# Two feed-forward layers behind a retention layer: the place of g's remainder in layer 1, and who copies the finished sums

## The chip, the cores and the metric

The kernel runs on one core of one Trainium2 chip. The metric is the device time of one execution in microseconds (us). Before the change it was 1250.7 us, the median of three runs from 1245.84 to 1251.95. TensorE (PE in the rows; PEld is its loading of weights), VectorE (DVE), ScalarE (ACT) and GpSimd (POOL) work side by side, each through its own list of instructions in order; all transfers of this kernel are issued by SyncE (SP).

## The reference, cut to what matters

```python
def _attn_ref(q, k, v):                      # batch 4, heads 8, seq 768, head_dim 64
    for t in range(S):
        state = gamma * state + einsum('bhd,bhe->bhde', k[:, :, t], v[:, :, t])
        y[:, :, t] = scale * einsum('bhd,bhde->bhe', q[:, :, t], state)

def _moe_ref(x, w_in, w_out, a, b):          # layer 1: 3072 tokens, 512 -> 2048 -> 512
    h = x @ w_in
    P = a[0] + a[1] * h + a[2] * h2 + a[3] * h3
    Q = 1.0 + abs(b[0]) * abs(h) + abs(b[1]) * h2
    g = P / (Q + 1e-06)
    return g @ w_out

def _moe2_ref(x, w_in, w_out):               # layer 2: the same sizes
    h = x @ w_in
    g = h * clip(h + 3.0, 0.0, 6.0) / 6.0
    return g @ w_out

out = _moe2_ref(_moe_ref(attn_out))
```

## The kernel before, in words

The 3072 tokens are cut into six blocks of 512. The retention layer (`att_*`) is computed in chunks of 128 tokens and runs in between layer 1. Each of the two feed-forward layers goes through its hidden units in 16 tiles of 128 (`f`). One **step** is one layer, one block and one tile: `emit_h` makes h, 128 hidden units x 512 tokens, in one PSUM bank; VectorE and ScalarE make g from it; `emit_o` multiplies g with the tile of `w_out` and adds to four PSUM banks, which are the halves of the tiles `accA` and `accB`. Layer 1 is `layer == 0` in the code, layer 2 is `layer == 1`.

All numbers are split into a part that TensorE's fp32r format holds exactly and the rest: x into `xh` and `xl`, weights into `wh` and `wl`, g into `gh` and `gl`. A product is the sum of three: high x high, high x low, low x high. So h takes 12 matmuls of 128x512 (4 slices of the input x 3), and the output takes 12 (4 banks x 3). ScalarE makes `gh` (`s_hi`, L416); VectorE makes `gl` = g - `gh` (`s_lo`, L422).

g of layer 1 takes the following. ScalarE makes three functions of h (`s1_h`, L388 to L390: `p`, `s`, `u`). VectorE makes `p` x h, then `u`, then a last `p` from h (`s1_pq`, L396 to L398). ScalarE takes the logarithm and the exponential of `u` (`s1_r`, L403 and L404). VectorE makes g in three instructions (`s1_g`, L409 to L411). Layer 2 needs one instruction of each engine (L428, L434).

The order of all work is written out by hand in one loop over steps, and each engine keeps it. In turn n of the loop TensorE gets h of step n, then the output matmuls of step n-2; ScalarE and VectorE work on h of step n-1 and finish g of step n-2. Weights come by DMA, and their split is spread over the steps: ScalarE scales (`w_scale`, L110), VectorE takes the bits apart (`w_bits`, L115, L117, L120), ScalarE casts (`w_hi`, L127), VectorE subtracts (`w_lo`, L132). A chunk of retention adds its scores (`sc`, L205) on TensorE in one turn, the mask (`T` or `Tb`, L214) on VectorE and the matmuls `py` (L236 to L262) on TensorE in the next, and ScalarE's copy of `py` (`xh`, L292, or `xf`, L287) in the one behind that.

The steps are ordered in segments: in each layer the first 8 tiles of block 0, then all of block 1, the other 8 tiles of block 0, and blocks 2 to 5. A segment of block 0 leaves its sums in DRAM, and the other adds to them. At the end of a segment `emit_evac` copies the four banks out of PSUM (L365, L369, L371) and sends them to DRAM. Before the change the copies go to ScalarE and VectorE in turn, at the end of the turn of the loop, behind `gl`; and in layer 1 the output matmuls of that turn are held back and issued one turn later, together with the next ones:

```python
        wait = len(late) > 0 and late[0][0] == 0
        for key in late:
            emit_evac(*key)
```

## Time and profile before

| | us |
|---|---|
| median of three runs | 1250.7 |
| the profiled execution | 1249.73 |
| its span, first to last instruction | 1247.9 |
| TensorE busy (matmuls) | 1165.6 (93%) |
| VectorE busy | 837.2 (67%) |
| ScalarE busy | 602.2 (48%) |
| mean share of full TensorE clock | 0.978 |

The share of busy time is a mean over stretches that differ: the first 45 us are mostly transfers and the retention of block 0; up to about 720 us layer 1 runs, with retention beside it up to about 610; then layer 2. Weights are split from 18 to 235 us and from 620 to 830 us. One row of the chain of waits, followed back from the end, has TensorE with 70% of the span and VectorE with 18%. In a row of a timeline the number in brackets is the time in which the engine stood idle before the instruction, and behind the arrow what ended it.

### The profile page before, as it was taken

What the parts mean: (1) busy time and instruction counts of PE and PEld (TensorE: products, weight loads), DVE (VectorE), ACT (ScalarE), POOL (GpSimd) and SP (SyncE); (2) the same over time, 40 slices, a digit from 0 to 9 for tenths busy, and PEclk for the clock granted to TensorE, in tenths of its full rate; (3) what the DMA queues carried; (4) which work ended last, traced back from release to release, by engine and by line L of the source; (5) the groups of instructions that cost most, each with busy time, mean ns of one, the idle gap of its engine ahead of it and who ended that gap; (6) DMA issues with size and microseconds to landing.
All of it is one profiled execution on the core that took longest, in us unless ns stands there. A gap on an engine that the chain in (4) does not pass through costs nothing.

```text
span 1247.9 us, 15484 instructions
## 1 busy us (share of the span) xinstructions
PE 1165.6 (93%) x6022; PEld 940.6 (75%) x6022; DVE 837.2 (67%) x1293; ACT 602.2 (48%) x974; POOL 0.3 (0%) x6
## 2 busy tenths in 40 slices
PE   6677787999999999999989999999999999999998
PEld 4455565788788788778877778888888888888886
DVE  6899889889888888888899988753322223232322
ACT  2465556576566565666677655433222222222222
POOL 0000000000000000000000000000000000000000
PEclk9788899999999999999999999999999999999999
DMA  9633323140221211212122154312100100100000
GB/s 333 210 91 105 119 82 119 51 145 8 82 79 43 77 43 60 83 62 77 34 85 68 51 180 145 98 34 85 41 28 1 59 9 1 60 9 1 34 1 34
DMA packets 54650, 91.27 MB, mean 73 GB/s; under 512 B 4785, under 2 KB 23345, under 8 KB 54577
## 3 DMA queue, kind: packets, MB, share of 16 engines
q1 hardware_dynamic: 54576, 90.29, 22.0%
q8 instruction: 47, 0.77, 0.2%
q14 instruction: 27, 0.21, 0.1%
HBM read 74.54 MB, written 15.73 MB: 72 GB/s over the span
## 4 chain that ended last, share of the span: by engine, by line
PE 70%; DVE 18%; DMA 5%; ACT 4%; issue 2%; SPq 1%; ACTq 0%; DVEq 0%
PE h L317 32%; PE accB L340 17%; PE accA L340 17%; DVE p L396 2%; DVE u L409 2%; DVE p L410 2%; DVE p L411 2%; DVE u L397 2%; PE py L236 1%; DMA rwo<-in_moe_w_out_dram 1%; PE sc L205 1%; DVE rwi L117 1%; DVE gl L422 1%; DMA kv<-in_kv_dram 1%; DVE rwo L117 1%
## 5 line engine op out<-in xcount | busy, mean ns | idle before, releaser
L317 PE MATMUL h<-xh,wi 128*128 128x512 f32 x1536 | 511.6, 395 | 1.7 <-DVE p L398 1.0
L317 PEld LDWEIGHTS h<-xh,wi 128*128 128x128 f32 x1536 | 290.6, 189 | 68.2 <-issue 3.1
L317 PE MATMUL h<-xl,wi 128*128 128x512 f32 x768 | 300.6, 391 | 0.2 <-DVE xl L299 0.2
L434 DVE SCALAR_TENSOR_TENSOR g<-r,h 128x512 f32<-128x512 f32 x96 | 66.1, 689 | 164.5 <-ACT r L428 164.5
L317 PEld LDWEIGHTS h<-xl,wi 128*128 128x128 f32 x768 | 145.4, 189 | 30.0 <-DVE xl L299 0.5
L422 DVE TENSOR_TENSOR gl<-g,gh 128x512 fp32r<-128x512 f32 x96 | 66.4, 692 | 124.8 <-ACT gh L416 124.1
L428 ACT ACTIVATE r<-h,cst 128x512 f32<-128x512 f32 x96 | 66.0, 687 | 168.5 <-PE h L317 168.4
L416 ACT ACTIVATE gh<-g 128x512 fp32r<-128x512 f32 x96 | 60.7, 632 | 174.3 <-PE accB L340 172.2
L340 PE MATMUL accB<-gh,wo 128*128 128x512 f32 x384 | 141.0, 409 | 0.0
L340 PE MATMUL accA<-gh,wo 128*128 128x512 f32 x384 | 137.7, 400 | 1.7 <-ACT gh L416 1.7
L340 PE MATMUL accA<-gl,wo 128*128 128x512 f32 x192 | 80.9, 422 | 49.5 <-DVE gl L422 49.5
L340 PE MATMUL accA<-wo,gh 128*128 128x512 f32 x384 | 118.2, 389 | 0.0
L340 PE MATMUL accB<-wo,gh 128*128 128x512 f32 x384 | 118.2, 389 | 0.0
L403 ACT ACTIVATE r<-u,cst 128x512 f32<-128x512 f32 x96 | 69.3, 722 | 65.4 <-DVE u L397 65.4
L388 ACT ACTIVATE p<-h,ab 128x512 f32<-128x512 f32 x96 | 74.4, 775 | 51.2 <-PE h L317 47.6
L340 PEld LDWEIGHTS accA<-gl,wo 128*128 128x128 f32 x192 | 36.8, 192 | 70.5 <-DVE gl L422 63.8
L340 PEld LDWEIGHTS accB<-gh,wo 128*128 128x128 f32 x384 | 76.6, 200 | 17.1
L340 PEld LDWEIGHTS accA<-gh,wo 128*128 128x128 f32 x384 | 73.7, 192 | 17.1 <-ACT gh L416 2.8
L340 PEld LDWEIGHTS accB<-wo,gh 128*128 128x128 f32 x384 | 72.1, 188 | 15.1
L340 PEld LDWEIGHTS accA<-wo,gh 128*128 128x128 f32 x384 | 72.1, 188 | 14.9
L422 DVE TENSOR_TENSOR gl<-p,gh 128x512 fp32r<-128x512 f32 x96 | 65.9, 686 | 24.7 <-ACT gh L416 24.6
L340 PE MATMUL accB<-gl,wo 128*128 128x512 f32 x192 | 78.8, 410 | 0.0
(73 smaller groups left out, 1498.2 us busy)
## 6 DMA issues: line engine op xcount, KB each, us to landing
rwi<-in_moe_w_in_dram SPq DMA_DIRECT2D x32, 512.0 KB, 3.7
rwo<-in_moe_w_out_dram SPq DMA_DIRECT2D x32, 512.0 KB, 3.6
T<-in_qk_t_dram SPq DMA_DIRECT2D x32, 256.0 KB, 3.6
kv<-in_kv_dram SPq DMA_DIRECT2D x32, 256.0 KB, 4.6
x<-o SPq DMA_DIRECT2D x24, 256.0 KB, 2.3
xr<-x SPq DMA_DIRECT2D x24, 256.0 KB, 3.9
out_dram<-o SPq DMA_DIRECT2D x20, 256.0 KB, 2.2
Tr<-in_kv_dram SPq DMA_DIRECT2D x16, 256.0 KB, 6.1
```

The source lines that it names most:

```text
L117: nc.vector.tensor_scalar(out=halves[:, :, 1], in0=halves[:, :, 3], scalar1=-(2**15), scalar2=None, op0=ALU.bitwise_and)
L317: nc.tensor.matmul(ps, lhsT=w[:, cs], rhs=x[:, c, :], start=n == 0, stop=n == 3 * KD - 1)
L340: nc.tensor.matmul(ps, lhsT=l, rhs=r, start=f == f0 and i == 0, stop=f == f1 and i == 2)
L388: nc.scalar.activation(p, h, AF.Identity, scale=ab[:, 3:4], bias=ab[:, 2:3])
L396: nc.vector.tensor_tensor(out=p, in0=p, in1=h, op=ALU.mult)
L397: nc.vector.scalar_tensor_tensor(out=u, in0=s, scalar=babs[:, 1:2], in1=u, op0=ALU.mult, op1=ALU.add)
L403: nc.scalar.activation(r, u, AF.Ln, scale=1.0 / LN_SCALE, bias=ln_bias)
L409: nc.vector.scalar_tensor_tensor(out=u, in0=u, scalar=Q_CONST, in1=r, op0=ALU.add, op1=ALU.mult)
L416: nc.scalar.activation(gh, tm[key], AF.Copy)
L422: nc.vector.tensor_tensor(out=gl, in0=tm.pop(key), in1=gh.bitcast(F32), op=ALU.subtract)
L428: nc.scalar.activation(r, hps[key], AF.Relu, bias=three)
L434: nc.vector.scalar_tensor_tensor(out=g, in0=r, scalar=6.0, in1=h, op0=ALU.min, op1=ALU.mult)
```

## The change

Four things are altered.

- `emit_h`: the 12 matmuls run through the four slices of high x high first, then high weight x low x, then low weight x high x. Before, each slice had its three products together.
- `emit_o`: in layer 1 the matmuls run over all four banks with one product after the other, and those with `gl` come last. In the last step of a segment, and in layer 2, each bank still gets its three products together, but with `gl` as the third.
- `s1_pq` takes a function that it calls between `u` and the last `p`; in layer 1 this is `s_lo` of the step before, which used to come behind `s1_r`.
- In layer 1 all four copies are on ScalarE, emitted right behind `s1_h` (for a segment that adds to sums from DRAM they stay on VectorE, and are emitted behind `gh`). The holding back of output matmuls is gone.

TensorE's order at the turn in which step 4 of block 1 gets its output matmuls: `h_1_6` is h of step 6 in block 1, `accA` and `accB` are the four banks, `py_1` the retention matmuls of chunk 1. Before:

```order
L317 MATMUL h_1_6_1369<-xh_455,wi_6_685 128x512
L340 MATMUL accA_1_0_1226<-gh_1_4_1391,wo_4_629 128x512 [waits Activation_49]
L340 MATMUL accA_1_0_1226<-gl_1_4_1406,wo_4_629 128x512 [waits DVE_49]
L340 MATMUL accA_1_0_1226<-gh_1_4_1391,wo_4_629 128x512 x2
L340 MATMUL accA_1_0_1226<-gl_1_4_1406,wo_4_629 128x512
L340 MATMUL accA_1_0_1226<-gh_1_4_1391,wo_4_629 128x512
L340 MATMUL accB_1_0_1227<-gh_1_4_1391,wo_4_629 128x512
L340 MATMUL accB_1_0_1227<-gl_1_4_1406,wo_4_629 128x512
L340 MATMUL accB_1_0_1227<-gh_1_4_1391,wo_4_629 128x512 x2
L340 MATMUL accB_1_0_1227<-gl_1_4_1406,wo_4_629 128x512
L340 MATMUL accB_1_0_1227<-gh_1_4_1391,wo_4_629 128x512
L236 MATMUL py_1_1423<-T_1_1216,kv_1_1217 64x128 [waits DMAHW0_49,DVE_49]
```

The same turn after the change:

```order
L317 MATMUL h_1_6_1369<-xh_455,wi_6_685 128x512 x4
L341 MATMUL accA_1_0_1148<-gh_1_4_1391,wo_4_629 128x512 [waits Activation_49]
L341 MATMUL accA_1_0_1148<-gh_1_4_1391,wo_4_629 128x512
L341 MATMUL accB_1_0_1149<-gh_1_4_1391,wo_4_629 128x512 x2
L341 MATMUL accA_1_0_1148<-gh_1_4_1391,wo_4_629 128x512 x2
L341 MATMUL accB_1_0_1149<-gh_1_4_1391,wo_4_629 128x512 x2
L341 MATMUL accA_1_0_1148<-gl_1_4_1402,wo_4_629 128x512 [waits DVE_49]
L341 MATMUL accA_1_0_1148<-gl_1_4_1402,wo_4_629 128x512
L341 MATMUL accB_1_0_1149<-gl_1_4_1402,wo_4_629 128x512 x2
L236 MATMUL py_1_1423<-T_1_1230,kv_1_1231 64x128 [waits DMAHW0_49,DVE_49]
```

The first matmul that waits for `gl` (DVE) was the second of twelve, and is the ninth.

VectorE's order in the same turn, from the first instruction on h of step 5 to the mask. Before:

```order
L396 TENSOR_TENSOR p_5_1384<-p_5_1384,h_1_5_1307 128x512
L397 SCALAR_TENSOR_TENSOR u_5_1383<-s_5_1382,babs,u_5_1383 128x512
L398 SCALAR_TENSOR_TENSOR p_5_1384<-p_5_1384,ab,h_1_5_1307 128x512 [waits DVE_49]
L422 TENSOR_TENSOR gl_1_4_1406<-p_4_1322,gh_1_4_1391 128x512 [waits PE_49]
L214 TENSOR_TENSOR T_1_1216<-sc_1_1360,tab 128x1024 [waits DMAHW7_49,PE_49]
```

After the change:

```order
L397 TENSOR_TENSOR p_5_1384<-p_5_1384,h_1_5_1307 128x512
L398 SCALAR_TENSOR_TENSOR u_5_1383<-s_5_1382,babs,u_5_1383 128x512
L425 TENSOR_TENSOR gl_1_4_1402<-p_4_1322,gh_1_4_1391 128x512 [waits PE_49]
L401 SCALAR_TENSOR_TENSOR p_5_1384<-p_5_1384,ab,h_1_5_1307 128x512 [waits DVE_49]
L214 TENSOR_TENSOR T_1_1230<-sc_1_1360,tab 128x1024 [waits DMAHW7_49,PE_49]
```

`gl` has changed places with the last `p`; the mask `T_1` stands where it stood.

ScalarE's order around the end of the first segment, where `o_0_7_0` to `o_0_7_3` are the copies of the four banks, `p_1`, `s_1`, `u_1` the functions of h of step 1 in block 1, and `gh_1_0` the cast of g of step 0. Before:

```order
L388 ACTIVATE p_1_1109<-h_1_1_1032,ab 128x512 [waits DVE_49,PE_49]
L389 ACTIVATE s_1_1107<-h_1_1_1032 128x512
L390 ACTIVATE u_1_1108<-h_1_1_1032,ab 128x512
L416 ACTIVATE gh_1_0_1116<-p_0_1047 128x512 [waits DVE_49]
L110 ACTIVATE rwo_10_1071<-rwo_10_1071 128x512 [waits DMAHW6_49]
L127 ACTIVATE wo_10_1123<-rwo_10_1071 128x512 [waits DVE_49]
L403 ACTIVATE r_1_1128<-u_1_1108,cst 128x512 [waits DVE_49,Activation_49]
L404 ACTIVATE r_1_1128<-r_1_1128 128x512 [waits Activation_49]
L369 ACTIVATE o_0_7_0_1133<-accA_0_0_552 128x512 [waits PE_49]
L369 ACTIVATE o_0_7_2_1139<-accB_0_0_553 128x512 [waits PE_49]
L388 ACTIVATE p_2_1188<-h_1_2_1094,ab 128x512 [waits DVE_49,PE_49]
```

After the change:

```order
L389 ACTIVATE p_1_1109<-h_1_1_1032,ab 128x512 [waits DVE_49,PE_49]
L390 ACTIVATE s_1_1107<-h_1_1_1032 128x512
L391 ACTIVATE u_1_1108<-h_1_1_1032,ab 128x512
L370 ACTIVATE o_0_7_0_1113<-accA_0_0_552 128x512 [waits PE_49]
L370 ACTIVATE o_0_7_1_1116<-accA_0_0_552 128x512
L370 ACTIVATE o_0_7_2_1119<-accB_0_0_553 128x512 [waits PE_49]
L370 ACTIVATE o_0_7_3_1122<-accB_0_0_553 128x512 [waits DMAHW7_49,Activation_49]
L419 ACTIVATE gh_1_0_1128<-p_0_1047 128x512 [waits DVE_49]
L110 ACTIVATE rwo_10_1071<-rwo_10_1071 128x512 [waits DMAHW6_49]
L127 ACTIVATE wo_10_1135<-rwo_10_1071 128x512 [waits DVE_49]
L406 ACTIVATE r_1_1142<-u_1_1108,cst 128x512 [waits DVE_49]
L407 ACTIVATE r_1_1142<-r_1_1142 128x512 [waits Activation_49]
```

Two copies behind the exponential have become four behind the functions of h, in front of the cast `gh_1_0` and of the scaling of the next weight.

```diff
--- before.py
+++ after.py
@@ -310,12 +310,11 @@
         ps = ps_h.tile([128, 512], F32, tag="h", name=f"h{layer}_{blk}_{f}")
         wh, wl = weights["wi", layer, f]
         xh, xl = xin[blk + layer * NBLK]
-        n = 0
-        for c in range(KD):
+        pairs = ((wh, xh), (wh, xl), (wl, xh))
+        for n, (i, c) in enumerate((i, c) for i in range(3) for c in range(KD)):
+            w, x = pairs[i]
             cs = slice(c * 128, (c + 1) * 128)
-            for w, x in ((wl, xh), (wh, xl), (wh, xh)):
-                nc.tensor.matmul(ps, lhsT=w[:, cs], rhs=x[:, c, :], start=n == 0, stop=n == 3 * KD - 1)
-                n += 1
+            nc.tensor.matmul(ps, lhsT=w[:, cs], rhs=x[:, c, :], start=n == 0, stop=n == 3 * KD - 1)
         hps[key] = ps
 
     def emit_o(key):
@@ -329,15 +328,17 @@
                 for t in (ps_acc.tile([128, 1024], F32, tag=f"acc{s}", name=f"acc{s}{layer}_{blk}_{f}") for s in "AB")
                 for i in range(2)
             ]
-        for j in range(KD):
+
+        parts = [(i, j) for i in range(3) for j in range(KD)]
+        if layer == 1 or f == f1:
+            parts.sort(key=lambda t: t[1])
+        for i, j in parts:
             js = slice(j * 128, (j + 1) * 128)
-            ps = acc[layer, blk][j]
             if layer == 0:
-                terms = ((wl[:, js], gh), (wh[:, js], gl), (wh[:, js], gh))
+                l, r = ((wh[:, js], gh), (wl[:, js], gh), (wh[:, js], gl))[i]
             else:
-                terms = ((gl[:, js], wh), (gh[:, js], wl), (gh[:, js], wh))
-            for i, (l, r) in enumerate(terms):
-                nc.tensor.matmul(ps, lhsT=l, rhs=r, start=f == f0 and i == 0, stop=f == f1 and i == 2)
+                l, r = ((gh[:, js], wh), (gh[:, js], wl), (gl[:, js], wh))[i]
+            nc.tensor.matmul(acc[layer, blk][j], lhsT=l, rhs=r, start=f == f0 and i == 0, stop=f == f1 and i == 2)
 
     partial = {}
 
@@ -365,7 +366,7 @@
                 nc.vector.scalar_tensor_tensor(out=o, in0=ps, scalar=scale, in1=o, op0=ALU.mult, op1=ALU.add)
             else:
                 o = out_tile(layer, blk, j, f"o{layer}_{blk}_{f}_{j}")
-                if j % 2 == 0:
+                if layer == 0 or j % 2 == 0:
                     nc.scalar.activation(o, ps, AF.Copy, scale=scale)
                 else:
                     nc.vector.tensor_scalar(out=o, in0=ps, scalar1=scale, scalar2=None, op0=ALU.mult)
@@ -390,11 +391,13 @@
         nc.scalar.activation(u, h, AF.Abs, scale=ab[:, 4:5])
         tm[key] = [s, u, p]
 
-    def s1_pq(key):
+    def s1_pq(key, between=None):
         s, u, p = tm[key]
         h = hps.pop(key)
         nc.vector.tensor_tensor(out=p, in0=p, in1=h, op=ALU.mult)
         nc.vector.scalar_tensor_tensor(out=u, in0=s, scalar=babs[:, 1:2], in1=u, op0=ALU.mult, op1=ALU.add)
+        if between:
+            between()
         nc.vector.scalar_tensor_tensor(out=p, in0=p, scalar=ab[:, 1:2], in1=h, op0=ALU.add, op1=ALU.mult)
 
     def s1_r(key):
@@ -630,7 +633,7 @@
                 if fn is not att_load:
                     begun.append((fn, *args))
 
-    late, held_back = [], []
+    late = []
     for n in range(len(steps) + LAG):
         cur, k1, k2 = (at_step(n - i) for i in range(3))
         todo = w_until(n) - made["bits"]
@@ -641,6 +644,9 @@
         begun.clear()
         if k1:
             (s1_h, s2_h)[k1[0]](k1)
+        for key in late:
+            if key[:2] not in partial and key[0] == 0:
+                emit_evac(*key)
         for fn, *args in begin.get(n, ()):
             fn(*args)
         if k2 and k2[0] == 0:
@@ -648,23 +654,23 @@
             s_hi(k2)
         elif k2:
             s_lo(k2)
+        for key in late:
+            if key[:2] in acc:
+                emit_evac(*key)
+        late.clear()
         while made["lo"] < made["bits"]:
             w_second()
+        rest = (lambda: s_lo(k2)) if k2 and k2[0] == 0 else None
         if k1 and k1[0] == 1:
+            if rest:
+                rest()
             s2_g(k1)
             s_hi(k1)
         if todo > 0:
             w_first()
         if k1 and k1[0] == 0:
-            s1_pq(k1)
+            s1_pq(k1, rest)
             s1_r(k1)
-        if k2 and k2[0] == 0:
-            s_lo(k2)
-
-        wait = len(late) > 0 and late[0][0] == 0
-        for key in late:
-            emit_evac(*key)
-        late.clear()
         if todo > 1:
             w_second()
         for fn, *args in before.get(n, ()):
@@ -680,13 +686,9 @@
         w_ahead(NW if n < N1 - FT else 2 * NW)
         o = at_step(n - LAG)
         if o:
-            held_back.append(o)
-        if not wait:
-            for o in held_back:
-                emit_o(o)
-                if o[2] == ends[o][1]:
-                    late.append(o)
-            held_back.clear()
+            emit_o(o)
+            if o[2] == ends[o][1]:
+                late.append(o)
         for fn, *args in after.get(n, ()):
             fn(*args)
         if cur and cur[1:] == (0, FT - 1):
```

## Rows read from the trace of the kernel before

**Rows 1.** Busy time in six stretches: length, PE, PEld, DVE, ACT, POOL, clock, DMA

```profile
40.00:127.00 87.00, 63.68 (x355) 47.63 (x348) 82.50 (x134) 50.55 (x84) 0.00 (x0) 0.85 0.37 116
127.00:227.00 100.00, 77.36 (x450) 59.47 (x449) 83.95 (x134) 57.71 (x95) 0.00 (x0) 0.94 0.35 109
227.00:613.00 386.00, 379.88 (x2216) 307.03 (x2215) 330.74 (x504) 239.92 (x389) 0.00 (x0) 1.00 0.20 65
613.00:721.00 108.00, 97.95 (x410) 76.63 (x408) 101.79 (x162) 76.55 (x126) 0.00 (x0) 0.98 0.20 62
721.00:767.00 46.00, 45.40 (x193) 37.40 (x194) 39.69 (x65) 25.78 (x44) 0.00 (x0) 0.96 0.48 164
767.00:1248.00 481.00, 476.15 (x2100) 393.62 (x2098) 169.16 (x254) 142.25 (x225) 0.00 (x0) 1.00 0.11 37
```

**Rows 2.** Waits over the whole span: us in total, times, longest us

```profile
PE accA L340 <- DVE gl L422: 49.5, 29, 3.6
```

**Rows 3.** TensorE's waits from 300 to 600 us

```profile
PE accA L340 <- DVE gl L422: 6.1, 6, 1.3
```

**Rows 4.** VectorE's waits from 127 to 227 us

```profile
DVE rwi L117 <- ACT rwi L110: 6.5, 5, 3.4
```

**Rows 5.** Timeline, 178 to 188 us: start, length, engine, line, what, [idle before]

```profile
178.84 0.74 DVE L398 SCALAR_TENSOR_TENSOR p<-p,ab,h 128x512 f32<-128x512 f32 x1
...
179.50 0.68 DVE L422 TENSOR_TENSOR gl<-p,gh 128x512 fp32r<-128x512 f32 x1
...
180.10 1.22 DVE L214 TENSOR_TENSOR T<-sc,tab 128x1024 f32<-128x1024 f32 x1
...
183.71 1.09 PE L236 MATMUL py<-T,kv 128*64 128x128 f32 x16
...
185.93 0.60 ACT L287 ACTIVATE xf<-py 128x512 f32<-128x512 f32 x1 [2.99 <-PE py L262]
...
187.64 0.76 DVE L117 TENSOR_SCALAR rwi<-rwi 128x512 int16<-128x512 int16 x1 [3.40 <-ACT rwi L110]
```

**Rows 6.** Timeline, 215 to 223 us

```profile
215.70 1.22 DVE L214 TENSOR_TENSOR T<-sc,tab 128x1024 f32<-128x1024 f32 x1
...
220.78 0.60 ACT L287 ACTIVATE xf<-py 128x512 f32<-128x512 f32 x1 [3.05 <-PE py L262]
...
222.50 0.75 DVE L117 TENSOR_SCALAR rwo<-rwo 128x512 int16<-128x512 int16 x1 [2.65 <-ACT rwo L110]
```

**Rows 7.** Timeline, 134 to 146 us, the first end of a segment

```profile
134.23 0.76 ACT L388 ACTIVATE p<-h,ab 128x512 f32<-128x512 f32 x1
...
137.72 0.74 DVE L117 TENSOR_SCALAR rwo<-rwo 128x512 int16<-128x512 int16 x1 [0.34 <-ACT rwo L110]
...
141.84 0.58 ACT L369 ACTIVATE o<-accA 128x512 f32<-128x512 f32 x1
...
142.31 0.59 ACT L369 ACTIVATE o<-accB 128x512 f32<-128x512 f32 x1
...
142.45 0.69 DVE L371 TENSOR_SCALAR o<-accA 128x512 f32<-128x512 f32 x1 [0.74 <-ACT o L369]
...
144.56 0.69 DVE L371 TENSOR_SCALAR o<-accB 128x512 f32<-128x512 f32 x1 [1.42 <-DMA x<-o]
...
145.17 1.21 DVE L214 TENSOR_TENSOR T<-sc,tab 128x1024 f32<-128x1024 f32 x1
```

**Rows 8.** DMA issues: what, count, KB each, median us to landing

```profile
x<-o SPq DMA_DIRECT2D x24, 256.0 KB, 2.3
```

**Rows 9.** Timeline at 226.55 us

```profile
226.55 0.50 PE L340 MATMUL accA<-gl,wo 128*128 128x512 f32 x1 [2.65 <-DVE gl L422]
```

**Rows 10.** The stretch right behind it, columns as in rows 1

```profile
228.00:231.40 3.40, 3.40 (x9) 2.63 (x9) 3.37 (x7) 1.69 (x3) 0.00 (x0) 0.50 0.00 0
```

**Rows 11.** Timeline at the change of layers, 720 to 722 us

```profile
720.87 0.68 DVE L422 TENSOR_TENSOR gl<-p,gh 128x512 fp32r<-128x512 f32 x1
...
721.61 0.50 PE L340 MATMUL accA<-gl,wo 128*128 128x512 f32 x1 [2.36 <-DVE gl L422]
```

## Prediction

> **What bounds the kernel now.** I read the stretches first [rows 1]. Five of them count here. From 40 to 227 us VectorE sets the pace: it is busy 82.5 of 87 us and then 84.0 of 100 us, while TensorE is busy only 63.7 and 77.4. (Neighbouring VectorE instructions overlap by some 0.08 us, so these sums are a little high: 179.50 + 0.68 against a next start of 180.10 [rows 5].) From 227 to 613 TensorE is busy 379.9 of 386 us and sets the pace. From 613 to 721 VectorE does so again, with 101.8 of 108 us. From 721 on TensorE is close to full, and after 767 it is full: 2100 matmuls in 481 us, which is 0.229 us for one. In that last stretch nothing can be gained except by doing fewer matmuls, and the change keeps their number.
>
> Then the waits: TensorE waits 49.5 us in 29 places for `gl`, the rest of g [rows 2], but only 6.1 us of that lies in 300 to 600 [rows 3]. This is the main reading. Where VectorE has no idle time, TensorE's wait is only the other side of VectorE's work, and letting TensorE run past it shortens nothing until VectorE waits in turn for something that TensorE hands over. So I do not count the 49.5 us; I look for places where VectorE itself stands still, and for the places where the pace goes from VectorE to TensorE.
>
> **The change part by part.** Three edits act together in layer 1. (a) In every step but the last of a segment, the output matmuls take `gl` as the last 4 of 12 and no longer as the second. (b) `gl` is made one VectorE instruction earlier, ahead of the third function of h. (c) The finished sums are copied by ScalarE alone, right behind the functions of h, and the next output matmuls are no longer held back by a step. The number of matmuls, and of VectorE instructions in a step without an end, stays. The new order inside h costs nothing that I can see: TensorE never waits there for a weight's low half. At each of the six whole ends of layer 1 two copies leave VectorE, and two are added on ScalarE.
>
> *40 to 127 us.* VectorE is full and nothing is taken from it. Gain 0.
>
> *127 to 227 us.* Here VectorE does wait, mainly for ScalarE's scaling of the next weight; the costliest group of its waits there is 6.5 us in 5 [rows 4]. The long ones come from one chain: `gl`, the output matmuls, the retention matmuls `py` behind them, ScalarE's copy `xf` of `py`, then ScalarE's cast of g and the scaling. At 187.64 VectorE stands 3.40 us for it [rows 5]. By (b) `gl` starts 0.66 us earlier (178.84 to 179.50), and by (a) 4 instead of 11 matmuls are left behind it, which is 7 x 0.229 = 1.60 us. Together 2.26 us, if nothing else holds `py`. The mask `T` is the other input: it starts at 180.10, is 1.22 us long and so ends at 181.32, and `py` starts at 183.71, so there are 2.39 us of room and all 2.26 count. At the second such place [rows 6] the mask ends at 215.70 + 1.22 = 216.92, and `py`, which takes as long as before (183.71 to 185.93, 2.22 us), started at 220.78 - 2.22 = 218.56. There only 1.6 us can be had; I take 1.35 of them for the start of a matmul behind a wait. Sum 3.6.
>
> The first end lies here too [rows 7]. Today VectorE stands behind the copies, 1.42 us of it for a transfer to leave an output buffer, and the mask starts only at 145.17. After the change the four copies stand on ScalarE between the functions of h (from 134.23, about 2 us long) and the cast of g. Two copies start 0.47 us apart, so four take 1.9 us, and the fourth must wait until the first one's transfer has landed, 2.3 us behind its issue [rows 8], about 1.7 us more than its turn. The scaling behind them, and with it VectorE's 137.72, come some 2.7 us later than now. In exchange VectorE is rid of the 1.42 us, of 0.74 us in front of its first copy and of two copies that hold it for 0.6 us each: 3.4 us. Net 0.7 us, and `py` no longer runs in front of a held-back output step. I take 1.2, between 0 and 3.
>
> *227 us, where the pace goes over to TensorE.* From 226.55 on TensorE runs without a wait; it starts there behind 2.65 us of waiting [rows 9]. With 8 of the 12 matmuls done before `gl` it has a lead of 2.26 us over today. VectorE must follow through the next steps; it has idle time there, but not at once. I take 1.9. Right behind it TensorE has its clock at half (0.50, the level of 1.2 GHz) for 3.4 us [rows 10], which costs 1.7 us; in front of the fall it had waited 2.65 us. A shorter wait may spare the fall.
>
> *227 to 613 us.* Only the waits count: 6.1 us in 6 places [rows 3], two at the beginning of each block of tokens, all of them from copies on VectorE and the step held back. With the copies on ScalarE, finished 1.9 us behind the functions of h, and 1.6 us of new room for `gl`, I take all of them away, and the slow start behind each (about 0.1 us): 6.5. The cover for the copies is `py`, for which ScalarE waits at these three ends anyway. Without that cover, 3 x 1.9 = 5.7 us of them return.
>
> *613 to 721 us.* VectorE paces. At the end in this stretch two copies leave it, but the four on ScalarE hold up the scaling for which it waits. I take 0, between -1 and 2.
>
> *721 us, the change of layers.* `gl` of the last step now stands behind a weight's conversion and starts at 720.87; TensorE waits 2.36 us for it and goes on at 721.61 [rows 11]. After the change `gl` of this step comes before that conversion (three instructions) and the next layer's g. Four VectorE instructions of about 0.6 us make 2.4 us, of which I take 2.2 because the cast of g has to be ready, and one more matmul is done before `gl`. From there TensorE has hardly a wait, so 2.5 us are kept. A mean clock of 0.96 in the next 46 us [rows 1] is another 1.8 us that may be spared.
>
> For the two falls of the clock together (1.7 + 1.8) I count a quarter, 0.9. Sum: 3.6 + 1.2 + 1.9 + 6.5 + 0 + 2.5 + 0.9 = 16.6. The profiled execution took 1249.7 us (span 1247.9 and 1.8 around it), 1.0 below the median of the runs. 1249.7 - 16.6 = 1233.1, forecast **1233**.
>
> **Rivals.** *The gain stays in the TensorE-paced part.* VectorE eats what the chains give back, because each stretch it paces ends when its own work ends. Then only 6.5 stay: 1249.7 - 6.5 = 1243. For it speaks that VectorE is busy 84 to 95% in these stretches; against it the 3.40 us idle, which can't be VectorE's work.
>
> *All waits for `gl` go.* 1249.7 - 49.5 = 1200. Against it stands that VectorE has only 4.5 us free of 87 between 40 and 127, and 6.2 of 108 between 613 and 721, so the TensorE waits there have nowhere to go.
>
> *The copies hold up ScalarE (slower).* Place: the six ends. Price: 1.9 us each in front of the cast of g, and 1.7 once for the landing, 13.1 us. It decides if the copies end later than TensorE reaches the next output matmuls, two groups of 12 (5.5 us) behind the end of h. Then the terms 1.2, 6.5 and 2.5 are lost as well and only 3.6 and 1.9 stay: 1249.7 - 5.5 + 13.1 = 1257. Against it: the functions of h and four copies are together about 4 us, below the 5.5.
>
> *The rotation over four banks lowers the clock (slower).* Today six matmuls in a row go to accA, six to accB, and TensorE's clock is 1.00 over 227 to 613 [rows 1]; afterwards each matmul of an output step in layer 1 goes to another bank than the one before. If that left gaps and took the clock to the 0.94 of 127 to 227, some 6% of 386 us would be lost: 1249.7 - 10.1 + 23 = 1263. No row shows a gap where accB follows accA. The Trainium skill (TensorE: Matmul & The Clock Gate, section on a second HAM failure mode) reports a kernel that cycles through PSUM banks each iteration and whose clock went back and forth because of small idle times between groups. By that rule this rival would be the likely one; the trace of before, which already uses four banks in each step at a clock of 1.00, doesn't bear it out.
>
> *The change doesn't do what it says:* if `gl` were late by more than the 1.6 us everywhere, the result would lie within 1249 to 1251.
>
> **How the numbers follow.** Forecast 0.68, gain only in the TensorE-paced part 0.16, all waits 0.03, copies hold up ScalarE 0.07, banks and clock 0.03, no effect 0.03. The forecast's own terms run from 12 (first end 0, handover 1, no clock, a second chain at 1) to 24 us (both falls spared, first end 3, 613 to 721 at 2), that is 1226 to 1238. Taking in the first rival the range is 1224 to 1244. About 0.5% (6 us) is what a measurement can tell from no change. Faster by more: nearly all of the forecast, two thirds of the first rival and all of the second, 0.81. Within 0.5%: 0.11. Slower: 0.08.
>
> **What would show it.** In the profile after, the six `gl` waits of TensorE between 300 and 600 us should be nearly gone, and VectorE's wait at about 187 should be near 1.1 us. The stretch from 40 to 127 should be as long as now. TensorE should go on at the change of layers some 16 us earlier. No ScalarE copy should be the last thing that VectorE or TensorE waits for, except once at the first end. It is wrong if ScalarE's cast of g shows up as what TensorE waits for, if the clock falls inside 227 to 613, or if VectorE's idle time between 127 and 227 stays at its sum.

## The result, and the profile after

The changed kernel takes 1231.07 us (median of four runs, 1229.19 to 1232.37), the kernel before 1249.84 in the same runs. The ratio is 0.9849 (95% interval 0.9828 to 0.987): 18.8 us less. The profiled execution took 1232.37 us, with a span of 1230.6.

Where the time went is read best from the turns of the loop. A turn is taken to begin where ScalarE starts its first function of h (`p`, or `r` in layer 2); the table subtracts these starts. For the changed kernel there are two profiles, the second of them from the experiments. A segment's end, where sums are copied, is called an end; a `py` chain is the way from `gl` over the output matmuls and `py` to the scaling of the next weight; the handover is the place near 227 us where the pace goes from VectorE to TensorE.

| turns | in before, us | length before | after | after, second profile | gain | predicted |
|---|---|---|---|---|---|---|
| up to turn 0 | 0 to 41 | 40.74 | 43.43 | 40.55 | -2.69 (+0.19) | - |
| 0 to 8 | 41 to 127 | 86.40 | 86.32 | 86.38 | 0.08 | 0 |
| 8 to 11, the first end | 127 to 156 | 28.75 | 26.40 | 26.40 | 2.35 | 1.2 |
| 11 to 19, two `py` chains | 156 to 227 | 70.73 | 67.32 | 66.83 | 3.41 | 3.6 |
| 19 to 24, the handover | 227 to 259 | 32.00 | 29.06 | 29.08 | 2.94 | 1.9 and clock |
| 24 to 80 | 259 to 613 | 354.49 | 346.21 | 346.21 | 8.28 | 6.5 |
| 80 to 96 | 613 to 717 | 103.41 | 103.66 | 103.74 | -0.25 | 0 |
| 96 to 108, the change of layers | 717 to 784 | 67.36 | 64.16 | 64.18 | 3.20 | 2.5 |

From turn 108 on both have 451.52 us to their last step. The gains sum to 20.0; less the 2.69 us by which the first profile reached turn 0 later, that is 17.3, the difference of the spans.

TensorE's waits over the whole span, the lines that answer to [rows 2] (us in total, times, longest):

```profile
PE accA L341 <- DVE gl L425: 25.6, 22, 2.8
PE py L236 <- DVE Tb L214: 15.3, 8, 4.4
PE accA L341 <- ACT gh L419: 13.8, 11, 3.4
```

`gl` fell from 49.5 to 25.6 us. From 300 to 600 us, where [rows 3] has 6.1 us, no wait of TensorE is listed any more. What is left lies where VectorE paces, and there part of it only changed its name: TensorE now stands at `gh`, the cast, 13.8 us (1.7 before).

The stretches, with the columns of [rows 1]:

```profile
40.00:127.00 87.00, 64.56 (x393) 47.93 (x392) 82.51 (x134) 50.11 (x83) 0.00 (x0) 0.90 0.36 115
227.00:613.00 386.00, 384.36 (x2249) 312.72 (x2248) 331.69 (x509) 253.05 (x410) 0.00 (x0) 1.00 0.20 67
613.00:721.00 108.00, 99.83 (x416) 77.43 (x416) 102.60 (x164) 76.01 (x126) 0.00 (x0) 0.98 0.26 83
```

VectorE is as busy in the first and third as before (82.5 and 101.8). In the second TensorE has gone from 379.9 to 384.4 of 386 us, with a clock of 1.00.

The first `py` chain, to set beside [rows 5]:

```profile
179.25 0.68 DVE L425 TENSOR_TENSOR gl<-p,gh 128x512 fp32r<-128x512 f32 x1
179.85 0.74 DVE L401 SCALAR_TENSOR_TENSOR p<-p,ab,h 128x512 f32<-128x512 f32 x1
180.51 1.21 DVE L214 TENSOR_TENSOR T<-sc,tab 128x1024 f32<-128x1024 f32 x1
...
181.81 1.09 PE L236 MATMUL py<-T,kv 128*64 128x128 f32 x16
...
184.03 0.60 ACT L287 ACTIVATE xf<-py 128x512 f32<-128x512 f32 x1 [1.49 <-PE py L262]
...
185.73 0.75 DVE L117 TENSOR_SCALAR rwi<-rwi 128x512 int16<-128x512 int16 x1 [1.07 <-ACT rwi L110]
```

VectorE's wait is 1.07 in place of 3.40 us. The mask `T` ends at 180.51 + 1.21 = 181.72 and `py` starts at 181.81: the mask is now what `py` waits for, as the row of its weight load says:

```profile
181.81 0.85 PEld L236 LDWEIGHTS py<-T,kv 128*64 128x64 f32 x16 [0.35 <-DVE T L214]
```

The first end, to set beside [rows 7]:

```profile
138.51 1.09 ACT L370 ACTIVATE o<-accA 128x512 f32<-128x512 f32 x2
140.74 1.09 ACT L370 ACTIVATE o<-accB 128x512 f32<-128x512 f32 x2 [1.14 <-PE accB L341]
141.73 0.62 ACT L419 ACTIVATE gh<-p 128x512 fp32r<-128x512 f32 x1
142.25 0.65 ACT L110 ACTIVATE rwo<-rwo 128x512 f32<-128x512 f32 x1
...
142.93 0.75 DVE L117 TENSOR_SCALAR rwo<-rwo 128x512 int16<-128x512 int16 x1 [2.99 <-ACT rwo L110]
```

VectorE stands 2.99 us for the scaling behind the four copies; ScalarE stands 1.14 us between the second and the third because `accB` was not done. The transfer that held up an output buffer before [rows 7] no longer shows. `accB` was late because TensorE stood for `gl` in the output step of this end and then ran at half its clock. The kernel before waits as long there, and its clock stays full. Before, then after, each with the stretch around it (columns of [rows 1]):

```profile
134.16 0.50 PE L340 MATMUL accA<-gl,wo 128*128 128x512 f32 x1 [2.69 <-DVE gl L422]
134.00:138.50 4.50, 4.34 (x29) 3.40 (x30) 3.84 (x8) 3.27 (x6) 0.00 (x0) 1.00 0.00 0
```

```profile
136.07 0.79 PE L341 MATMUL accA<-gl,wo 128*128 128x512 f32 x1 [2.69 <-DVE gl L425]
136.00:140.50 4.50, 4.43 (x10) 3.14 (x10) 3.66 (x7) 3.57 (x7) 0.00 (x0) 0.50 0.12 45
```

VectorE stands as long at the end near 605 us, where a weight is split in the same turn (1.21 us before, at 621.49):

```profile
609.08 0.76 DVE L117 TENSOR_SCALAR rwi<-rwi 128x512 int16<-128x512 int16 x1 [3.17 <-ACT rwi L110]
```

The change of layers [rows 11], and the clock there:

```profile
704.49 0.69 DVE L425 TENSOR_TENSOR gl<-p,gh 128x512 fp32r<-128x512 f32 x1
704.51 0.73 PE L341 MATMUL accA<-gh,wo 128*128 128x512 f32 x2 [1.84 <-ACT gh L419]
```

```profile
705.00:709.00 4.00, 4.00 (x12) 3.01 (x11) 3.78 (x7) 2.54 (x5) 0.00 (x0) 0.57 0.38 131
```

TensorE resumes 17.1 us earlier than in [rows 11], and waits for the cast, no longer for `gl`. The clock still falls to half there. The fall behind the handover [rows 10] is gone; the one at the first end is new.

### The profile page after: what moved, and what is told of

It is laid out like the page before. It is cut to its first block, busy times and chain, and to the rows that moved or that the text cites. A ratio compares the mean times of both kernels' runs of the same rounds, so it can differ in the third digit from the quotient of the medians.

```text
span 1230.6 us, 15579 instructions
## 1 busy us (share of the span) xinstructions
PE 1161.1 (94%) x6022; PEld 937.6 (76%) x6022; DVE 826.4 (67%) x1281; ACT 609.8 (50%) x986; POOL 0.3 (0%) x6
## 4 chain that ended last, share of the span: by engine, by line
PE 76%; DVE 16%; ACT 4%; issue 2%; DMA 2%; SPq 0%; ACTq 0%; DVEq 0%
PE h L317 35%; PE accA L341 18%; PE accB L341 18%; PE py L236 2%; PE sc L205 2%; DVE p L397 2%; DVE u L398 2%; DVE u L412 1%; DVE p L413 1%; DMA rwo<-in_moe_w_out_dram 1%; DVE rwi L117 1%; DVE p L414 1%; DVE rwo L117 1%; PE py L262 1%; DVE p L401 1%
## 5 line engine op out<-in xcount | busy, mean ns | idle before, releaser
L317 PE MATMUL h<-xh,wi 128*128 128x512 f32 x1536 | 417.8, 394 | 0.7 <-ACT xh L292 0.7
L317 PEld LDWEIGHTS h<-xh,wi 128*128 128x128 f32 x1536 | 286.6, 189 | 65.0 <-issue 3.4
L317 PE MATMUL h<-xl,wi 128*128 128x512 f32 x768 | 206.4, 391 | 0.0
L341 PE MATMUL accA<-gh,wo 128*128 128x512 f32 x384 | 122.0, 399 | 13.8 <-ACT gh L419 13.8
L341 PE MATMUL accB<-gh,wo 128*128 128x512 f32 x384 | 121.0, 397 | 0.0
L341 PE MATMUL accA<-gl,wo 128*128 128x512 f32 x192 | 64.4, 411 | 25.6 <-DVE gl L425 25.6
L341 PEld LDWEIGHTS accB<-gh,wo 128*128 128x128 f32 x384 | 73.6, 192 | 15.9
L419 ACT ACTIVATE gh<-p 128x512 fp32r<-128x512 f32 x96 | 60.7, 632 | 34.5 <-DVE p L414 34.4
L341 PE MATMUL accA<-wo,gl 128*128 128x512 f32 x192 | 74.8, 390 | 0.0
```

Source lines behind the costliest of these rows:

```text
L317: nc.tensor.matmul(ps, lhsT=w[:, cs], rhs=x[:, c, :], start=n == 0, stop=n == 3 * KD - 1)
L341: nc.tensor.matmul(acc[layer, blk][j], lhsT=l, rhs=r, start=f == f0 and i == 0, stop=f == f1 and i == 2)
L419: nc.scalar.activation(gh, tm[key], AF.Copy)
```

## The experiments

Four kernels undo one part of the change each, three make one part alone, one repeats the changed kernel, three go further, and one leaves work out.

**gl second of twelve again** (layer 1):

```diff
-        if layer == 1 or f == f1:
-            parts.sort(key=lambda t: t[1])
+        parts.sort(key=lambda t: t[1])
...
-                l, r = ((wh[:, js], gh), (wl[:, js], gh), (wh[:, js], gl))[i]
+                l, r = ((wl[:, js], gh), (wh[:, js], gl), (wh[:, js], gh))[i]
```

> The changed kernel, but in layer 1 the output matmuls again take the three products of a bank together, with gl second of twelve; the earlier gl and the copies on ScalarE stay. Theory (gl's place among the matmuls counts where a chain runs through them, not between 227 and 613 us): in the trace after, gl is ready 2.4 to 4.3 us before TensorE needs it between 264 and 600 us, and 7 x 0.229 = 1.60 us of that go, so no wait returns there. Back come 1.6 us at each of the two py chains before 227 us (3.2), 1.9 at the handover and perhaps the half-speed clock behind it (up to 1.7), 0.2 at the layer change: 5 to 7 us slower than the changed kernel's 1231, so 1236 to 1238. Rival 1 (the place does the work between 227 and 613 as well): the 6.5 us return too, 1243 to 1245. Rival 2 (the earlier gl and the copies do it all): 1231.

1234.11 us, ratio to the kernel before 0.9873 (0.9851 to 0.9896). Turns 24 to 80 stay at 346.21, so rival 1 falls. The handover costs 2.31 us, and the wait and the half clock are back:

```profile
225.36 0.50 PE L340 MATMUL accA<-gl,wo 128*128 128x512 f32 x1 [1.98 <-DVE gl L424]
```

```profile
227.00:230.40 3.40, 3.40 (x10) 2.64 (x9) 3.37 (x6) 1.69 (x4) 0.00 (x0) 0.52 0.17 66
```

The two chains cost 0.93 and 0.92 us by their turns (13 and 14, 17 and 18), not 3.2 together: the earlier `gl` and the copies cover the rest. The first end costs 1.37 us (turns 8 to 11). The change of layers is 1.34 us shorter than in the changed kernel: the clock does not fall there (1.00 from 705 to 709 us). So the median is 3.0 us above the changed kernel's, less than I expected.

**gl made late again:**

```diff
-            s1_pq(k1, rest)
+            s1_pq(k1)
             s1_r(k1)
+        if k2 and k2[0] == 0:
+            s_lo(k2)
```

(and the call of `rest()` at the change of layers goes.)

> The changed kernel, but gl is made where it was: behind the last p and, at the change of layers, behind the weight's conversion. Theory: 0.66 us return at the first py chain, at most 0.6 at the second, 0.7 at the handover, and 2.2 at the change of layers: 3.5 to 4.5 us slower than the changed kernel, about 1235. No wait of TensorE for gl between 300 and 600. Rival (the order of the matmuls alone does it, and gl's place on VectorE counts for nothing): 1231 to 1232.

1234.3 us, 0.9883 (0.9859 to 0.9907). 2.28 us return at the change of layers and 0.68 at the first end, nothing at the handover. At the first chain `py` starts 1.06 us into its turn instead of 1.09: no loss. At the second it starts 1.77 in instead of 1.08: 0.69, as the 0.66 of `gl`'s place.

**Copies and held-back step as before:** the old `emit_evac`, its old place and `held_back` are put back in.

> The changed kernel, but the finished sums are again copied by ScalarE and VectorE in turn at the end of the turn, and the output matmuls behind an end are held back by a turn. The prediction's step (the copies on VectorE and the held-back step make the waits between 300 and 600; without them they go): 4 to 6.5 us return there and about 2 at the first end, 1237 to 1240. Rival (the 2.26 us of room that gl has won cover these waits of 0.75 to 1.29 us by themselves, so copies and order each do the same work twice over): between 227 and 613 nothing returns, only the first end's 0 to 2.5 us, so 1231 to 1234.

1236.51 us, 0.9898 (0.9877 to 0.9919). 2.18 us return at the first end, 3.03 between turns 24 and 80. That is neither expectation. No wait for `gl` returned between 296 and 613 us; another did:

```profile
PE accA L341 <- ACT gh L419: 1.7, 4, 0.9
```

With `gl` out of the way the cast is late next. Two of the four waits (0.19 and 0.27 us, at 317 and 323) come behind VectorE's copies, from which it works without a pause to g. In front of the other two (0.92 at 426 and 0.37 at 527) VectorE last stood for transfers of the retention's inputs, 0.24 and 0.67 us the one time, 0.47 the other; the changed kernel shows no such wait between 296 and 600 us.

**The old order inside h:** only the loop in `emit_h` is put back.

> The changed kernel, but the 12 matmuls of h are in their old order (the three products of a slice together). Theory: nothing depends on it, 1231. Rival (the new order of h costs the 2.7 us by which the changed kernel's profile reaches its first step later, 43.43 against 40.74 us): 1228 to 1229, and the first step starts near 40.7 us again.

1230.26 us, 0.9848 (0.9823 to 0.9873), the same as the changed kernel within the noise. Its first turn starts at 43.61, so the rival falls.

**The changed kernel again.**

> The changed kernel once more, on the same chip as the three below. Its median should lie within 1229 to 1233. Question beside it: is the later first step (43.43 us instead of 40.74) part of the change or variation? Theory (variation: the code up to there is the same but for the order of h): the first step starts anywhere between 40.5 and 44 us. Rival (part of the change): 43 to 44 us again.

1231.54 us (1229.21 to 1232.88), 0.9847 (0.9828 to 0.9865). Turn 0 starts at 40.55: the start is variation.

**One part alone, added to the kernel before:** the order of the output matmuls, the copies, or `gl`'s place.

> The kernel before with one part of the change: in layer 1 the output matmuls run over the four banks and gl comes last (and gl third in each bank elsewhere). gl's place on VectorE, the copies and the held-back step are as before. Theory (each part covers what another would cover too): between 227 and 613 us 4 to 5 us go, because 1.6 us of room are more than each of the waits of 0.75 to 1.29; 2.5 to 3.5 us at the chains in 127 to 227, 2.3 at the handover, nothing at the first end, 0 to 0.4 at the change of layers: 9 to 11 us in all, so about 1240. Rival (the parts add up: what the order gives alone is what its absence cost, 3.0 us): about 1247.

> The kernel before with the other part: copies by ScalarE alone right behind the functions of h, no held-back step; gl second of twelve and made late, the matmuls in their old order. Theory (each part covers what another would cover too): the whole 8 us between 227 and 613 go, because without the copies VectorE never falls behind; 1.5 to 2.5 at the first end; 0 to 1.5 at the chains; nothing at the handover; -1 to 1 at the change of layers: 9 to 12 us in all, about 1239. Rival (the parts add up: what its absence cost, 5.4 us): about 1244. Rival 2 (the copies on ScalarE hold up the cast of g when gl has no room): slower than 1247.

> The kernel before with gl's new place on VectorE alone (between u and the last p, and ahead of the weight's conversion at the change of layers); matmuls and copies as before. Undone in the changed kernel it cost 3.2 us, 2.3 of them at the change of layers. Theory (0.66 us earlier counts wherever nothing else covers it): six waits of TensorE between 300 and 600 us shrink by 0.66 us each, 4.0; 0.66 at each of the two py chains; 0.7 at the handover; 2.3 at the change of layers: 7 to 9 us, 1241 to 1243. Rival (the place counts at the change of layers alone): 2 to 3 us, about 1247.

| us gained against before, by profile | all | order alone | place alone | copies alone | all but order | all but place | all but copies |
|---|---|---|---|---|---|---|---|
| turns 8 to 11 | 2.35 | -0.26 | -0.31 | 0.19 | 0.98 | 1.67 | 0.17 |
| 11 to 19 | 3.41 | 3.45 | 2.06 | 0.76 | 2.08 | 3.81 | 3.65 |
| 19 to 24 | 2.94 | 2.90 | 1.89 | 0.00 | 0.63 | 2.91 | 2.93 |
| 24 to 80 | 8.28 | 4.68 | 2.14 | 8.28 | 8.28 | 8.27 | 5.25 |
| 96 to 108 | 3.20 | 0.51 | 2.59 | 2.27 | 4.54 | 0.92 | 3.22 |
| median, us | 1231.07 | 1240.01 | 1243.95 | 1242.24 | 1234.11 | 1234.3 | 1236.51 |

Their ratios are 0.9915 (0.9899 to 0.9931), 0.9952 (0.9934 to 0.997) and 0.993 (0.9915 to 0.9945). The three medians alone are 10.4, 6.3 and 8.1 us below the kernel before in their own runs, 24.8 together against 18.8 for the whole; undone one at a time they cost 3.0, 3.2 and 5.4, or 11.7. The parts cover for one another: 10.4 us for the order is the theory's figure, not the 3.0 of simple adding up; the copies (8.1) lie between the 9 to 12 of the theory and the 5.4 of adding up, the place just short of its 7 to 9. (One execution can differ from the median of its kernel by 2 to 3 us, so the stage sums don't give the medians.) In turns 24 to 80, where the clock is 1.00 throughout, the covering is plain: the copies alone take everything. With the place alone the waits between 296 and 613 us only shrink, and a new name appears:

```profile
PE accA L341 <- DVE gl L425: 3.2, 6, 0.7
PE accA L341 <- ACT gh L419: 0.4, 1, 0.4
```

At the first end no part alone does anything. The copies count there together with another part, 1.67 us with the order and 0.98 with the place, and all three give 2.35.

Two rows of the table hold the clock too. At the change of layers it falls in the kernel before, in the changed one, in order alone and in all but place; in the other four it doesn't. The copies alone gain 2.27 us there with TensorE's wait as it was and the fall missing:

```profile
713.53 0.50 PE L341 MATMUL accA<-gl,wo 128*128 128x512 f32 x1 [2.33 <-DVE gl L425]
714.00:718.00 4.00, 4.00 (x20) 3.28 (x19) 3.07 (x6) 2.89 (x7) 0.00 (x0) 1.00 0.40 146
```

The kernel before, behind its 2.36 us [rows 11]:

```profile
722.00:726.00 4.00, 4.00 (x13) 3.16 (x12) 3.13 (x6) 0.58 (x2) 0.00 (x0) 0.61 0.00 0
```

At the handover the clock falls in the kernel before, in copies alone and in all but order. With the place alone it doesn't, behind the same wait as in all but order (1.98):

```profile
227.03 0.50 PE L341 MATMUL accA<-gl,wo 128*128 128x512 f32 x1 [1.96 <-DVE gl L425]
228.40:231.80 3.40, 3.40 (x17) 2.81 (x16) 3.37 (x7) 1.82 (x4) 0.00 (x0) 1.00 0.20 75
```

These two kernels differ in turns 19 to 24 by 1.89 - 0.63 = 1.26 us. They have different copies, which alone give 0.00 there, and a different order inside h, which changes nothing there (29.06 and 29.11 us). So, as an estimate, some 1.3 us of the gain at the handover are the fall that is spared. Whether a kernel shows a fall in every execution was not measured; the changed kernel's two profiles agree.

(In turns 11 to 19 some 0.5 us differ between executions of one kernel, by when a weight's transfer lands: VectorE's wait for it in turn 11 is 0.85 in one profile of the changed kernel and 0.38 in the other.)

**Copies behind the scaling** where a weight is split in the same turn:

```diff
+                if todo > 0:
+                    emit_evac(*key, range(2 if key[1] == 0 else 0))
+                    copies = lambda key=key: emit_evac(*key, range(2 if key[1] == 0 else 0, KD))
...
         w_scale_next(i + 2)
+        if copies:
+            copies()
         w_hi(*jobs[i])
```

> The changed kernel, but at the two ends where a weight is split in the same turn (the first end, and the one at 605 us) copies are moved behind gh and the scaling of that weight: the last two of four at the first end, all four at the other. In the trace after, VectorE waits 2.99 us and 3.17 us there for the scaling, in stretches that VectorE paces. Theory (VectorE's standstill behind the copies is lost time): VectorE's waits fall to about 1.9 and 1.2, and the time falls by 2 to 4 us, to 1227 to 1229. Rival (TensorE is behind at these places anyway, so the waits only move): same time as the changed kernel on this chip.

1229.37 us, 0.9833 (0.9816 to 0.9849); the medians differ by 2.2 us, but the intervals overlap. By profile 1.8 us go at the end near 605 (3.17 becomes 1.21). At the first end the wait moved a turn on, and turns 8 to 11 stay at 26.28 us:

```profile
142.79 0.75 DVE L117 TENSOR_SCALAR rwo<-rwo 128x512 int16<-128x512 int16 x1 [0.75 <-ACT rwo L110]
...
154.00 0.75 DVE L117 TENSOR_SCALAR rwi<-rwi 128x512 int16<-128x512 int16 x1 [3.15 <-ACT rwi L110]
```

**gl last at the ends too**, on top of that: `if layer == 1 or f == f1:` becomes `if layer == 1:`.

> The kernel with the copies behind the scaling (the run before), and gl last over all four banks in the last step of a segment of layer 1 too. In the trace of the run before, VectorE's standstill at the first end went from 2.99 to 0.75 us, but 3.15 us came in the next turn, for a scaling that waits for the retention matmuls py; TensorE had stood 2.69 us at the ending step's gl with 8 matmuls ready that need no gl, and then ran 12 matmuls, scores, h and an output step without a pause up to py. Theory (TensorE's lateness at the first end is that order): 2 to 2.8 us go in the turns 8 to 11, nothing between 227 and 613, 0 to 1 at the change of layers; 1226 to 1228 where the changed kernel has 1231.5. Rival (the copies, which can begin only when all banks are done, hold up gh and the scaling by what is won): 1229 to 1230.

1227.66 us (1225.41 to 1228.08), 0.982 (0.9803 to 0.9837), the fastest kernel here. Turns 8 to 11 are 24.16 us, 2.24 below the changed kernel, and both waits are short:

```profile
140.72 0.75 DVE L117 TENSOR_SCALAR rwo<-rwo 128x512 int16<-128x512 int16 x1 [0.74 <-ACT rwo L110]
...
149.83 0.75 DVE L117 TENSOR_SCALAR rwi<-rwi 128x512 int16<-128x512 int16 x1 [1.04 <-ACT rwi L110]
```

**The rest of each weight on GpSimd**, on top of that:

```diff
-        nc.vector.tensor_tensor(out=lo, in0=z, in1=hi.bitcast(F32), op=ALU.subtract)
+        nc.gpsimd.tensor_tensor(out=lo, in0=z, in1=hi.bitcast(F32), op=ALU.subtract)
```

> The kernel of the run beside this one, with the last step of each weight's split (the rest of the weight, one VectorE instruction of 0.6 us) given to GpSimd, which is idle. 15 of these lie in the stretch from 40 to 127 us and 16 between 613 and 721. Theory (VectorE paces these stretches): if GpSimd works beside it, they get shorter by 0.6 us for each, 9 us each at the most, 1210 to 1222. The Trainium skill (SBUF — State Buffer, section on the two separate sides) says that VectorE's instructions with two SBUF inputs and GpSimd's lock each other out; no row of these traces shows GpSimd at such work. Rival, by that mechanism (each GpSimd instruction stops VectorE for about its own length, 0.6 us or more): no gain or slower, 1227 to 1245, and VectorE's instructions with two SBUF inputs get longer in the trace.

1246.59 us, 0.9981 (0.997 to 0.9993), 18.9 us slower than the kernel it starts from. Turns 0 to 8 take 93.15 us instead of 86.34, turns 11 to 19 73.90 instead of 66.75. From its timeline at 68 us:

```profile
68.59 1.62 POOL L132 TENSOR_TENSOR wi<-rwi,wi 128x512 fp32r<-128x512 f32 x1 [3.27 <-ACT wi L127]
```

```profile
68.32 0.74 DVE L401 SCALAR_TENSOR_TENSOR u<-s,babs,u 128x512 f32<-128x512 f32 x1
68.98 1.78 DVE L428 TENSOR_TENSOR gl<-p,gh 128x512 fp32r<-128x512 f32 x1
70.68 0.73 DVE L404 SCALAR_TENSOR_TENSOR p<-p,ab,h 128x512 f32<-128x512 f32 x1
```

`gl` takes 1.78 us instead of 0.68 and ends 0.55 us behind GpSimd's subtraction (70.76 and 70.21). The same befalls the last instruction of g once a turn. So about 2 x 1.1 us are lost in a turn with two weights and 2 x 0.6 saved: 1 us, as turn 1 shows (11.76 became 12.80). The rival is what happened.

**Without the matmuls of gl:**

```diff
+        if layer == 0 and f < f1:
+            parts = [t for t in parts if t[0] < 2]
```

> The changed kernel without the four matmuls with gl in the steps of layer 1 that end no segment: this part of the product is left out, and TensorE has 4 x 0.227 = 0.9 us less to do in each of these steps. Theory (VectorE paces 40 to 127 and 613 to 721 us, TensorE 227 to 613): the first 8 steps stay at 86.4 us and the steps from 613 on at 103.7 (each within 1 us), while the 48 steps in between lose up to 45 x 0.9 = 40 us, less where VectorE comes to pace them too (it is busy 332 of 386 us). Rival (TensorE paces with its waits everywhere): the first 8 steps lose 6 to 7 us and the last 16 about 13.

One run, 1188.74 us. Turns 0 to 8 take 86.28 us, turns 80 to 96 103.06, turns 24 to 80 306.56: 0.04, 0.60 and 39.65 us less than with these matmuls. TensorE's work counts between 259 and 613 us and hardly in the other two. In turns 11 to 19 the kernel with less work is 1.52 us slower (68.84). Its TensorE stands 3.62 us for the mask in front of the first `py`, its clock is 0.83 in the turns of both `py` chains (1.00 in the changed kernel), and VectorE waits 1.81 and 1.86 us for the scaling instead of 1.07 and 1.06:

```profile
179.27 1.09 PE L236 MATMUL py<-T,kv 128*64 128x128 f32 x16 [3.62 <-DVE T L214]
```

## Why the prediction was right, step by step

*40 to 127 and 613 to 721 us, gain 0.* Right: 0.08 and -0.25 in turns 0 to 8 and 80 to 96. Shown twice: work taken from TensorE shortens these turns by 0.04 and 0.60 us, and 1 us a turn added to VectorE lengthens the first by 6.8.

*The `py` chains, 3.6.* The sum was right (3.41 and 3.90 in the two profiles), its split was not, so that it fits is in part luck. By turns 13 and 14 the first chain gave 2.32 us (19.06 to 16.74), by turns 17 and 18 the second 1.58 (18.32 to 16.74). I counted 0.66 us of the first for `gl`'s new place and 1.60 for the order. The order alone gives all of the first (2.30), and the 2.39 us of room that I had read in front of the mask is used up: `py` starts 0.09 us behind it. At the second chain, where I counted nothing for the place, its 0.66 us are real: without it `py` starts 0.69 us later in the turn.

*The first end, 1.2 (0 to 3).* 2.35 measured. I saw that the copies would hold up the scaling, by 2.7 us; VectorE waits 2.99. I put this down partly to a transfer out of an output buffer. The waiting was for TensorE's `accB`, whose last matmuls came late: in a segment's last step `gl` stays third of twelve, TensorE stood 2.69 us for it, and behind that the clock was 0.50, a fall that the sum did not have. The further kernels show the first: moving the copies moved the wait, and `gl` last there took another 2.12 us off (26.28 to 24.16). TensorE no longer stands for `gl` at that end then, so how much of this is the order and how much the clock was not separated.

*The handover, 1.9, and a quarter of two clock falls, 0.9.* 2.94 in turns 19 to 24. The order gives it alone (2.90), and without it 0.63 are left; but `gl`'s place alone gives 1.89, since its clock does not fall. With 1.26 us for the fall, the lead that I put at 1.9 came to about 1.7, and the fall that I put at 1.7 cost less. That this fall went entirely was a quarter's chance; the other stayed in the changed kernel, and another came at the first end, which I had not counted.

*227 to 613 us, 6.5.* The mechanism was right and the size low: 8.28. The term that I mis-sized is what a wait costs. In the kernel before TensorE started a matmul at 321.61 us and the next, which waited, at 323.17, 1.56 us later instead of 0.227: 1.33 lost, where the profile writes 1.17, since it counts from the modelled end 0.39 us after the start. The one behind it came 0.34 us later, 0.11 more than the pace. So this wait cost 0.28 us above its listing; at six waits that is 1.7, and 6.1 + 1.7 = 7.8 of the 7.96 us in turns 32 to 80. (I had put 0.1 us on each, which makes 6.7 and not the 6.5 that I wrote.) The rows:

```profile
321.61 0.39 PE L340 MATMUL accA<-gh,wo 128*128 128x512 f32 x1
323.17 0.50 PE L340 MATMUL accA<-gl,wo 128*128 128x512 f32 x1 [1.17 <-DVE gl L422]
323.51 0.62 PE L340 MATMUL accA<-gh,wo 128*128 128x512 f32 x2
```

I also named two causes as if both were needed. The copies alone suffice; the order alone takes 4.68, and the rest turns into waits for the cast.

*The change of layers, 2.5.* Turns 96 to 104 gave 2.59, and without `gl`'s new place 2.28 return (I had taken 2.2). The clock falls in all three of these kernels, so it is not in the difference. The 0.61 us in turns 104 to 108 were not in the sum.

*What should show.* One sign of being wrong came: ScalarE's cast of g is what TensorE waits for, 13.8 us in 11 places. Nine lie before 203 us, where VectorE paces, one (0.56 us) just behind the handover and one (1.84) at the change of layers; none lies between 300 and 600 us, and the gain came all the same. The sign was too wide: it did not say where the wait has to stand to cost time. The `gl` waits from 300 to 600 and VectorE's wait of 1.1 us came as said. Wrong was that a copy would be the last thing waited for at the first end alone: at 609.08 it is again.

*The rivals.* The gain did not stay in the TensorE-paced part: 8.7 us lie in turns 8 to 24. The waits for `gl` did not all go; in turns 0 to 8 and 80 to 96, where they stayed, it cost nothing (0.08 and -0.25), at the first end it did. What the copies held up on ScalarE showed at two ends and not at six: VectorE waits 2.99 and 3.17 us there, 0.34 and 1.21 before. The banks: in layer 1 now every matmul of an output step, but for a segment's last, goes to another bank than the one before, and the clock from 227 to 613 us is 1.00 with TensorE busy 384.36 of 386. The kernel of which the Trainium skill (TensorE: Matmul & The Clock Gate, section on a second HAM failure mode) tells cycled through PSUM banks in each iteration, and its clock went back and forth because TensorE was idle for short times between groups. Here no wait of TensorE is listed from 300 to 600 us, and its clock does not swing.

*The range.* The terms named for its upper end add up to 23.0 us (16.6 + 2.6 + 1.8 + 2), not 24; this changes nothing in the result.

## What to carry to other kernels

A wait of an engine that is not the pace is not lost time by itself (though its clock can fall behind it, as TensorE's did at the first end); look for where the pacing engine itself stands, and for the places where the pace changes hands. Parts of a change that shorten the same wait cover for one another: what each is worth must be measured both alone and left out (and the clock compared at the places where it falls), and the next input in line (here the mask, then the cast) ends the gain. Where copies share an engine with something that the pacing engine needs soon, put that in front of them.

## What had not been expected of the hardware

- A VectorE instruction with two SBUF inputs that starts while GpSimd subtracts is held until GpSimd is done: 1.78 us for `gl` in place of 0.68, ending 0.55 us behind it. One that had begun 0.27 us before GpSimd (`u`, 68.32) kept its 0.74. The Trainium skill (SBUF — State Buffer, section on the two separate sides) says that the one which starts first has the ports for its whole length; the trace agrees.
- The half clock does not follow from the wait in front of it alone. Three pairs of rows above show one wait with both outcomes: 2.69 us at the first end (1.00 before, 0.50 after), 2.36 and 2.33 at the change of layers (0.61 before, 1.00 with the copies alone), 1.98 and 1.96 at the handover (0.52 with `gl` second of twelve again, 1.00 with its place alone). A fourth: the changed kernel and the one with the old order of h both wait 1.8 us for `gh` at the change of layers, and 0.9 to 1.0 for `gl` some 6 us ahead of it; only the first shows the fall (0.57 over 705 to 709 us; the other 1.00 over 700 to 710), and turns 96 to 108 take 64.16 and 62.60 us. What decides it stays open.
- The start of turn 0 lies between 40.55 and 45.47 us in the profiles of these kernels, with nearly the same work before it: up to 4.9 us, 0.4% of the time, that no change made.
